# A hashed-attention and two-layer feed-forward kernel: two tiles for the compared bits, another first pair of PSUM banks, and six weight operations in other steps

## The chip, the cores and the metric

The kernel runs on one NeuronCore of one Trainium2 chip. The metric is the time of one execution in microseconds (us) on the device. PE is TensorE (matrix products and transposes), DVE is VectorE, ACT is ScalarE, POOL is GpSimd, and SP is the engine whose queue issues most of the transfers (DMAs). The unit of on-chip result memory that PE writes is a PSUM bank; there are eight.

## The reference

```python
# attention: q, k, v (2, 8, 768, 64), proj (64, 6)
q_bits = (np.einsum('bhsd,dk->bhsk', q, proj) > 0).astype(np.int64)
k_bits = (np.einsum('bhsd,dk->bhsk', k, proj) > 0).astype(np.int64)
powers = 2 ** np.arange(n_bits)
mask = q_bucket[:, :, :, None] == k_bucket[:, :, None, :]   # bucket = sum(bits * powers)
scores = np.where(mask, scale * np.matmul(q, k.transpose(0, 1, 3, 2)), -1000000000.0)
scores = scores - np.max(scores, axis=-1, keepdims=True)
attn = np.exp(scores)
attn = attn / (np.sum(attn, axis=-1, keepdims=True) + 1e-09)
attn_out = np.matmul(attn, v)
# x = attn_out as (1536, 512) tokens; two feed-forward layers, w_in (512, 2048), w_out (2048, 512)
x = np.maximum(x @ w_in, 0.0) ** 2 @ w_out
h = x @ w2_in
out = (h * (1.0 / (1.0 + np.exp(-h)))) @ w2_out
```

The weights of the feed-forward layers arrive as 64-bit floats and are turned into 32-bit floats on the chip.

## The kernel before

**Attention.** The 16 heads are taken as eight pairs (pair 0 to 7). A pair has two heads and each head's queries are taken in two halves of 384 rows, so there are four units `u` per pair and 32 in all. One unit is three blocks of 128 queries against 768 keys. The order of the work is written out by hand: a loop over a step `d` emits, for each step, the row maximum of one block of scores (`row_max`, L984, DVE), two tiny DVE operations (`row_live`, L988 and L989), six transposes of 128x128 into two PSUM tiles `t` (`transp`, L1013, PE), their rounding on ACT (`t_hi`, L1018) and the remainder on DVE (`t_lo`, L1024), four products with v (`av`, L1037 and L1038, PE), the exponential (L997, ACT), and the four products of the next block of scores (`score_mm`, L977, PE). One block of scores per step, so twelve steps per pair, and steps 0 to 95 hold the transposes.

**The bits.** The mask is added by the score product itself: 12 rows of sign bits per head stand below the 64 rows of q and k in the operand tiles `qq` and `kk`. For pair p = 2 to 7, with d0 = 12(p-1), the eight small products of the bits go into one tile `t` of PSUM at the end of step d0-2 (`bits_mm`, L786; this step also does one `t_lo` early). In step d0-1, right behind `row_live`, DVE compares them into the tile `bt` (`bits_cmp`, L791). Pair 1 has its compare in step 2. SP copies `bt` into `qq` and `kk` with four transfers for each head (`place_bits`, L910): for the first head in step d0+2, for the second in step d0+8. The scores use them from step d0+7 and d0+13. SP issues its transfers in order; each one also waits for the landing of the one eight before it. The tile `bt` has one buffer, and so the compare of pair p+1 (step d0+11) needs the last of the four transfers of pair p's second head to have landed. PSUM tiles `t` have three buffers; while the bits wait in one of them, the transposes of the second step behind them wait for it.

**The w_in tiles.** The first four tiles of the first layer's w_in (128x512 each, i = 0 to 3) are converted during the attention: a load (`w_load`), ACT's absolute value (`w_abs`), POOL's limits (`w_limit`), and three DVE operations: `w_exp` (L946), `w_sign` (L950) and `w_low` (L954). The table `W_STEPS` gives for each tile the steps of load, absolute value, `w_exp`, `w_sign` and `w_low`. The DVE operations stand in the list `mid[d]`, between `row_live` and the step's first `t_lo`. In the step of `w_low` of tiles 0 and 1, POOL splits the tile into two parts in `wpa` (`wp_put`, L961 and L962).

**The feed-forward layers.** `moe` records its operations in a planner with costs and due times, which sets the order on every engine; for PE it keeps the written order. The list `idle` hands out the PSUM banks, first in first out. Its first products (`plain`, L420) take 512 tokens at a time: four groups of 12 products, each group in a bank of its own, then the next 512 tokens. The eight tiles `bank0` to `bank7` lie over the attention's PSUM tiles: `bank0` and `bank1` over the first buffer of the scores tile `s`, `bank2` and `bank3` over the second, `bank4` to `bank6` over the `t` tiles and `bank7` over `o`. The last unit's output o31 is put into the first buffer of `s`, where DVE adds its two halves (L1045) at the very end of the attention. Behind the last products with v, PE makes six transposes of the last pair's row sums (L1277), and then the first L420 follows.

Of the kernel before, what the change touches and what calls it, by code (L numbers as in the profile page):

```python
# [11 lines left out]
F32 = mybir.dt.float32  # L12
F32R = mybir.dt.float32r
# [4 lines left out]
ALU = mybir.AluOpType  # L18
# [3 lines left out]
B, H, S, D = 2, 8, 768, 64  # L22
# [4 lines left out]
QW = 384  # L27
KT = S // 128
SCALE = D**-0.5
NBR = 2 * NB  # L30
# [7 lines left out]
W_LO = float(np.uint32(897 << 20).view(np.float32))  # L38
W_HI = float(np.uint32((1150 << 20) | 0xFFFFF).view(np.float32))
V_LAG = 4  # L40
W_STEPS = ((0, 5, 17, 29, 53), (8, 17, 41, 65, 77), (22, 29, 41, 92, 93), (54, 65, 92, 96, 96))
WA = 4
FB = 4
NP = FB // 2
# [175 lines left out]
def moe(nc, t):  # L220
# [11 lines left out]
        count[name] += 1  # L232
        return i

    idle = [0, 1, 4, 7, 2, 3, 5, 6]
    cells = list(range(NCELL))
    early = list(t["early"])

# [411 lines left out]
    for m in range(2):  # L650
        for f in range(NFB):
# [3 lines left out]
            elif m + f == 0:  # L655
                for h in range(2):
                    o = wpa[1][:, :, 4 * h : 4 * h + 4]
# [42 lines left out]
def lsh_attention_moe_moe(ctx, tc, kd, qk, qf, fq, v, pc, wi1, wo1, wi2, wo2, out):  # L700
    nc = tc.nc
# [16 lines left out]
    a1 = att.enter_context(tc.tile_pool(name="a1", bufs=1))  # L718
    a2 = att.enter_context(tc.tile_pool(name="a2", bufs=2))
# [11 lines left out]
    tm = [tmt[:, 2 * i : 2 * i + 2] for i in range(4)]  # L731
# [4 lines left out]
    pair = {}  # L736
# [50 lines left out]
        return o  # L787

    def bits_cmp(p, o):
        t = pair[p]["bt"] = a1.tile([128, S], F32R, tag="bt", name=f"bt{p}")  # L790
        nc.vector.tensor_scalar(out=t[:, 0:QW], in0=o[:, 0:QW], scalar1=tm[0][:, 0:1], scalar2=tm[0][:, 1:2], op0=ALU.is_gt, op1=ALU.mult)  # L791


    first = {}

# [108 lines left out]
    def place_bits(p, h):  # L904
        t = pair[p]
        for n, x in enumerate(("qq", "kk")):
            o = t[x][h][64 : 64 + NBR, 1, :].rearrange("r (z c) -> r z c", z=2)
            for z in range(2):
                r = 64 * n + 32 * z + NBR * h
                nc.sync.dma_start(out=o[:, z].bitcast(F32), in_=t["bt"][r : r + NBR, 0:QW].bitcast(F32))  # L910

    def load_v(p):
        t = pair[p]
# [196 lines left out]
    def at(g, fn, *a):  # L1110
        todo[g].append((fn, a))

    for p in range(1, NPAIR):
        d0 = 12 * (p - 1)
        if p > 1:
            at(d0 - 10, load_pair, p)
            at(d0 - 9, load_k, p)
            at(d0 - 4, new_hi, p)
            at(d0 - 4, cast_pair, p, 1)
            at(d0 - 3, split_pair, p, 1)  # L1120
            scale[d0 - 2] = p
            at(d0 - 2, cast_pair, p, 0)
            at(d0 - 1, split_pair, p, 0)
        else:
            at(0, split_pair, p, 0)
            at(0, split_pair, p, 1)
        long[max(d0 - 2, 1)] = p
        at(d0 + 1, load_head, p, 0)
        at(d0 + 2, place_lo, p, 0)
        at(d0 + 2, place_bits, p, 0)  # L1130
        at(d0 + 5, load_v, p)
        at(d0 + 8, split_v, p)
        at(d0 + 7, load_head, p, 1)
        at(d0 + 8, place_lo, p, 1)
        at(d0 + 8, place_bits, p, 1)
# [14 lines left out]
    for k, d in enumerate(X_STEPS):  # L1150
        at(d, x_form, k)
    for i, (d_load, d_abs, *d_dve) in enumerate(W_STEPS):
        key = (0, 0, i)
# [12 lines left out]
    with tc.manual_schedule():  # L1166
# [17 lines left out]
            out=pdx, in0=k[:, 0:NBR].unsqueeze(1).broadcast_to([128, 2, NBR]), in1=k[:, NBR : 3 * NBR].rearrange("p (a b) -> p a b", a=2), op=ALU.mult  # L1184
# [43 lines left out]
        for d in range(-5, G // 2 + 3):  # L1228
# [10 lines left out]
            if 0 <= g < G and d in (92, 94):  # L1239
                t = ps_s.tile([128, 2, 512], F32, tag="s", name=f"t{g}")  # L1240
# [25 lines left out]
            if d in long:  # L1266
                mid[d + 1].append((bits_cmp, (long[d], bits_mm(long[d]))))
# [5 lines left out]
        p = NPAIR - 1  # L1273
        for z in (1, 0):
            t = ps_t.tile([128, 512], F32, tag="t", name=f"rb{p}_{z}")
# [12 lines left out]
        t = dict(yf=yf, xk=xk, wpa=wpa, raw=raws, wt=wt, pair=both, src=((wi1, wo1), (wi2, wo2)), out=out)  # L1288
# [8 lines left out]
        ops = ("ACT", 0.68, w_abs), ("DVE", 0.43, w_limit), ("DVE", 0.43, w_exp), ("DVE", 0.7, w_sign), ("DVE", 0.7, w_low)  # L1297
        t["first"] = [[(eng, c, partial(fn, key)) for eng, c, fn in ops] for key in early]
        moe(nc, t).emit()


# [45 lines left out]
```

## Time and profile before

| what | value |
|---|---|
| three runs, median (lowest to highest) | 730.95 us (727.33 to 731.03) |
| the profiled execution, time and span | 731.64 us, span 729.9 us |
| mean granted TensorE clock | 0.995 of full speed |
| PE busy | 712.2 us (98%) |
| DVE, ACT, POOL busy | 604.9, 539.7 and 257.6 us |
| attention, until PE's last work of it | 0 to 234 us of the span |
| feed-forward layers | 236.6 us to the end |

A span is counted from the first instruction to the last. The times of rows are counted from the span's start. PE's busy time is modelled and counts overlapping matmuls, so that a high share doesn't say that PE runs at its peak; what PE loses is better read from the distance of equal instructions.

### The profile page before, as it was taken

To read this page: it belongs to the slowest core of one execution; us is meant where nothing else is said; L and a number is where in the kernel's file an instruction comes from. 1 tells how busy PE (TensorE), PEld (TensorE's weight loads), DVE (VectorE), ACT (ScalarE), POOL (GpSimd) and SP (SyncE) were. 2 spreads that over 40 slices of the span, in tenths; PEclk is the share of its full clock that TensorE was granted. 3 is DMA by queue.
4 is the path that set the end of the run, shared out by engine and by line. 5 is a ranking of instruction groups with operands and counts; after the bars stand their busy time and mean duration, and the time that the engine had idled before them with its cause. 6 is when DMAs were issued, how large, how long until landed. Compare 5 with 4: busy or idle time off the path is not lost.

```text
span 729.9 us, 10863 instructions
## 1 busy us (share of the span) xinstructions
PE 712.2 (98%) x3610; PEld 604.8 (83%) x3610; DVE 604.9 (83%) x1099; ACT 539.7 (74%) x1012; POOL 257.6 (35%) x239
## 2 busy tenths in 40 slices
PE   9999999979998999999999999999999999999998
PEld 4988988979897888888887888888788888888887
DVE  7989998969999879786887889989788788978840
ACT  6989998969897798477468558878766855864861
POOL 7635574555746503031232223145203210212300
PEclk9999999999999999999999999999999999999999
DMA  5767868758663337224535553378231331345432
GB/s 170 213 159 195 216 158 190 203 129 201 144 155 84 89 104 173 83 73 102 128 88 115 119 116 106 94 151 167 73 129 58 88 87 62 127 101 116 101 101 101
DMA packets 39496, 92.53 MB, mean 127 GB/s; under 512 B 5944, under 2 KB 11588, under 8 KB 39440
## 3 DMA queue, kind: packets, MB, share of 16 engines
q1 hardware_dynamic: 26976, 67.58, 31.6%
q0 software_dynamic: 12032, 23.79, 18.4%
q8 instruction: 29, 0.48, 0.3%
q10 hardware_dynamic: 432, 0.46, 0.2%
q14 instruction: 27, 0.22, 0.1%
HBM read 52.32 MB, written 3.19 MB: 76 GB/s over the span
## 4 chain that ended last, share of the span: by engine, by line
PE 77%; DVE 11%; SPq 4%; DMA 4%; issue 2%; ACT 1%; POOL 0%; DVEq 0%; ACTq 0%; POOLq 0%
PE bank L558 35%; PE bank L443 23%; PE bank L420 7%; DVE mt L984 4%; DVE tl L1024 4%; PE s L977 4%; PE t L1013 4%; DMA kk<-bt 2%; PE o L1037 2%; PE o L1038 2%; SPq L910 2%; DMA rx<-in_dram 1%; DMA cell<-cell 1%; SPq L766 1%; PE warm L968 1%
## 5 line engine op out<-in xcount | busy, mean ns | idle before, releaser
L558 PE MATMUL bank<-woh,cell 128*128 128x512 f32 (+1 forms) x392 | 120.0, 385 | 0.0
L558 PE MATMUL bank<-cell,woh 128*128 128x512 f32 x384 | 118.5, 389 | 0.2 <-DMA cell<-cell 0.2
L997 ACT ACTIVATE P<-s,mt 128x768 f32<-128x768 f32 x96 | 95.5, 995 | 12.1 <-DVE mt L989 10.3
L1024 DVE TENSOR_TENSOR tl<-t,th 128x384 fp32r<-128x384 f32 x192 | 104.1, 548 | 0.2
L984 DVE TENSOR_REDUCE mt<-s 128x1 f32<-128x768 f32 x96 | 91.3, 951 | 3.1 <-PE s L977 2.1
L1018 ACT CAST th<-t 128x384 fp32r<-128x384 f32 x192 | 82.7, 483 | 14.0 <-PE t L1013 13.9
L1013 PE MATMUL t<-ident,P 128*128 128x128 f32 x576 | 82.3, 276 | 9.7 <-DVE bt L791 8.3
L1013 PEld LDWEIGHTS t<-ident,P 128*128 128x128 f32 x576 | 67.5, 141 | 21.6 <-DVE bt L791 10.2
L558 PEld LDWEIGHTS bank<-woh,cell 128*128 128x128 f32 x392 | 73.2, 188 | 14.7
L558 PEld LDWEIGHTS bank<-cell,woh 128*128 128x128 f32 x384 | 72.1, 188 | 15.6 <-DMA cell<-cell 0.7
L977 PE MATMUL s<-kk,qq 76*128 76x384 f32 (+1 forms) x384 | 83.5, 339 | 0.5 <-ACT P L997 0.5
L278 DVE TENSOR_TENSOR cell<-bank,cell 128x512 f32<-128x512 f32 x91 | 62.1, 692 | 18.7 <-PE bank L443 14.4
L443 PE MATMUL bank<-xw,wpb 128*128 128x512 f32 x312 | 75.9, 389 | 0.0
L558 PE MATMUL bank<-wol,cell 128*128 128x512 f32 (+1 forms) x196 | 75.4, 385 | 0.0
L558 PE MATMUL bank<-cell,wol 128*128 128x512 f32 x192 | 74.7, 389 | 0.0
L1037 PE MATMUL o<-th,vv 128*128 128x384 f32 x192 | 73.1, 381 | 0.0
L977 PEld LDWEIGHTS s<-kk,qq 76*128 76x128 f32 (+1 forms) x384 | 68.1, 189 | 2.2 <-ACT P L997 1.6
L443 PEld LDWEIGHTS bank<-xw,wpb 128*128 128x128 f32 x312 | 58.5, 188 | 12.4 <-DVE bank L278 0.3
L1038 PE MATMUL o<-tl,vv 128*128 128x384 f32 x192 | 65.1, 339 | 0.0
L588 ACT COPY yf<-bank 128x512 f32<-128x512 f32 x48 | 27.9, 586 | 34.6 <-PE bank L558 34.0
L450 ACT COPY cell<-bank 128x512 f32<-128x512 f32 x39 | 22.9, 586 | 40.6 <-PE bank L443 38.6
L268 ACT CAST cell<-cell 128x512 fp32r<-128x512 f32 x81 | 48.8, 617 | 2.7 <-DMA cell<-cell 1.6
(185 smaller groups left out, 1456.0 us busy)
## 6 DMA issues: line engine op xcount, KB each, us to landing
raw<-in_dram SPq DMA_DIRECT2D x62, 512.0 KB
cell<-cell POOLq DMA_DIRECT2D x23, 256.0 KB, 4.0
qq<-hq SPq DMA_DIRECT2D x28, 192.0 KB
kk<-in_dram POOLq DMA_DIRECT2D x14, 384.0 KB, 4.5
yf<-cell POOLq DMA_DIRECT2D x21, 256.0 KB, 3.3
vr<-in_dram SPq DMA_DIRECT2D x8, 384.0 KB
ta<-ob SPq DMA_DIRECT2D x31, 96.0 KB
tb<-ob SPq DMA_DIRECT2D x31, 96.0 KB
```

What stands on the lines that cost most here:

```text
L278: add("DVE", 0.70, lambda: vec.tensor_tensor(out=val(out), in0=bank[b], in1=val(other), op=ALU.add), [("bank", b), *reads], writes)
L420: mm(bank[b], wpa[n][:, p, 4 * h + j], x[:, q], start=j == 0 and z == 0, stop=j == 3 and z == 2)
L443: mm(bank[b], w[:, p], x[:, q], start=not started and z == 0, stop=z == 2, skip_group_check=started)
L558: mm(bank[b][:, 0:wd], x, y, start=start and i == 0 and z == 0, stop=i == (FB if half is None else 2 * half + 2) - 1 and z == 2, skip_grou ...
L977: mm(s[:, n, 0:QW], t["qq"][h][0:kk, ab, c0 : c0 + 128], t["kk"][h][0:kk, ab, n * QW : (n + 1) * QW], start=ab == 0, stop=ab == 1)
L984: nc.vector.tensor_reduce(out=m[:, 0:1], in_=s[:, :, 0:QW], op=ALU.max, axis=AX.XY, negate=True)
L997: nc.scalar.activation(out=e.rearrange("p (a b) -> p a b", a=2), in_=s[:, :, 0:QW], func=AF.Exp, scale=m[:, 1:2], bias=m[:, 2:3], accum_ou ...
L1013: nc.tensor.transpose(t[:, j * 128 : (j + 1) * 128], P[u, j][:, kt * 128 : (kt + 1) * 128], ident)
L1018: nc.scalar.copy(out=th, in_=PT[g][0][:, 0:QW])
L1024: nc.vector.tensor_tensor(out=tl, in0=t[:, 0:QW], in1=th.bitcast(F32), op=ALU.subtract)
L1037: mm(o[:, 0:QW], vv, th, start=kt == 0, stop=False)
L1038: mm(o[:, 0:QW], vv, tl, start=False, stop=kt == KT - 1)
```

## The change

The compare writes tiles `bn` of 384 columns from a pool with two buffers, where it wrote the one buffer `bt` (768 columns, of which 384 were used). The list `idle` starts with banks 2 and 3 and has 0 and 1 in their place. Six DVE operations on the w_in tiles 0 and 1, and one on tile 2, stand in other steps; with `w_low`, the two operations of `wp_put` on POOL move as well. The loads, ACT's and POOL's first operations keep their steps.

```diff
-W_STEPS = ((0, 5, 17, 29, 53), (8, 17, 41, 65, 77), (22, 29, 41, 92, 93), (54, 65, 92, 96, 96))
+W_STEPS = ((0, 5, 10, 22, 34), (8, 17, 46, 58, 70), (22, 29, 46, 92, 93), (54, 65, 92, 96, 96))
...
-    idle = [0, 1, 4, 7, 2, 3, 5, 6]
+    idle = [2, 3, 4, 7, 0, 1, 5, 6]
...
     def bits_cmp(p, o):
-        t = pair[p]["bt"] = a1.tile([128, S], F32R, tag="bt", name=f"bt{p}")
-        nc.vector.tensor_scalar(out=t[:, 0:QW], in0=o[:, 0:QW], scalar1=tm[0][:, 0:1], scalar2=tm[0][:, 1:2], op0=ALU.is_gt, op1=ALU.mult)
+        t = pair[p]["bt"] = a2.tile([128, QW], F32R, tag="bn", name=f"bn{p}")
+        nc.vector.tensor_scalar(out=t, in0=o[:, 0:QW], scalar1=tm[0][:, 0:1], scalar2=tm[0][:, 1:2], op0=ALU.is_gt, op1=ALU.mult)
...
-                nc.sync.dma_start(out=o[:, z].bitcast(F32), in_=t["bt"][r : r + NBR, 0:QW].bitcast(F32))
+                nc.sync.dma_start(out=o[:, z].bitcast(F32), in_=t["bt"][r : r + NBR].bitcast(F32))
```

On DVE, this is the place of pair 2's compare (steps 10 and 11) before the change. In brackets stand the semaphores that an instruction waits for; DMAHW are those of SP's transfers.

```order
L1024 TENSOR_TENSOR tl20_631<-t20_625,th20_629 128x384 [waits Activation_49]
L1024 TENSOR_TENSOR tl21_647<-t21_633,th21_637 128x384 [waits Activation_49]
L984 TENSOR_REDUCE mt_92<-s5_0_651 128x1 [waits PE_49]
L988 TENSOR_SCALAR mt_92<-mt_92 128x1 [waits DVE_49]
L989 TENSOR_SCALAR mt_92<-mt_92 128x1
L791 TENSOR_SCALAR bt2_666<-bs2_656,tmt_88 128x384 [waits DMAHW3_49,DMAHW4_49,DMAHW2_49,DMAHW5_49,DMAHW1_49,PE_49]
L1024 TENSOR_TENSOR tl22_674<-t22_668,th22_672 128x384 [waits Activation_49]
```

The same place of DVE after the change (the lines behind L790 have a number that is lower by one), with `w_exp` of tile 0 ahead of step 10's remainders:

```order
L945 TENSOR_SCALAR wi0_288<-wi0_288 128x512 [waits Pool_49]
L1023 TENSOR_TENSOR tl20_632<-t20_626,th20_630 128x384 [waits Activation_49]
L1023 TENSOR_TENSOR tl21_648<-t21_634,th21_638 128x384 [waits Activation_49]
L983 TENSOR_REDUCE mt_92<-s5_0_652 128x1 [waits PE_49]
L987 TENSOR_SCALAR mt_92<-mt_92 128x1 [waits DVE_49]
L988 TENSOR_SCALAR mt_92<-mt_92 128x1
L791 TENSOR_SCALAR bn2_667<-bs2_657,tmt_88 128x384 [waits PE_49]
L1023 TENSOR_TENSOR tl22_675<-t22_669,th22_673 128x384 [waits Activation_49]
```

The compare now waits for PE alone (from pair 3 on also for transfers of two pairs before), and a w_in operation has come in six rows ahead of it; the same holds for the compares in steps 23, 35, 47, 59 and 71, with two such operations ahead of the one in step 47.

On PE, this is the place between the attention's last transposes (`rb`) and the first products of the feed-forward part before the change:

```order
L1277 MATMUL rb7_0_3739<-ident_86,rw7_3671 128x128 [waits PE_49]
L1277 MATMUL rb7_0_3739<-ident_86,rw7_3671 128x128 x2
L420 MATMUL bank0_3764<-xk_59,wpa0_60 128x512 [waits DVE_49]
L420 MATMUL bank0_3764<-xk_59,wpa0_60 128x512 x11
L420 MATMUL bank1_3765<-xk_59,wpa0_60 128x512 x12
L420 MATMUL bank4_3768<-xk_59,wpa1_61 128x512 [waits Activation_49]
L420 MATMUL bank4_3768<-xk_59,wpa1_61 128x512
L420 MATMUL bank4_3768<-xk_59,wpa1_61 128x512 [waits DVE_49]
L420 MATMUL bank4_3768<-xk_59,wpa1_61 128x512 x9
```

The same place of PE after the change:

```order
L1276 MATMUL rb7_0_3739<-ident_86,rw7_3671 128x128 [waits PE_49]
L1276 MATMUL rb7_0_3739<-ident_86,rw7_3671 128x128 x2
L420 MATMUL bank2_3766<-xk_59,wpa0_60 128x512 x12
L420 MATMUL bank3_3767<-xk_59,wpa0_60 128x512 x12
L420 MATMUL bank4_3768<-xk_59,wpa1_61 128x512 [waits PE_49,Activation_49]
L420 MATMUL bank4_3768<-xk_59,wpa1_61 128x512
L420 MATMUL bank4_3768<-xk_59,wpa1_61 128x512 [waits DVE_49]
L420 MATMUL bank4_3768<-xk_59,wpa1_61 128x512 x9
```

The first wait for DVE now stands 24 products later, at the weights of `wpa1`. In the rest of the feed-forward part the banks 0 and 2, and 1 and 3, have changed places; the order on every engine is otherwise the same.

## Rows read from the trace of the kernel before

**Rows 1.** The page: busy time, share of the span and instructions of each engine.

```profile
PE 712.2 (98%) x3610; PEld 604.8 (83%) x3610; DVE 604.9 (83%) x1099; ACT 539.7 (74%) x1012; POOL 257.6 (35%) x239
```

**Rows 2.** Waits, us in total, times, longest: DVE and PE in the attention.

```profile
DVE bt L791 <- DMA kk<-bt: 10.4, 5, 4.5
PE t L1013 <- DVE bt L791: 8.3, 6, 3.9
```

**Rows 3.** Timeline of PE, steps 10 to 14: start, length, instruction; idle before in brackets.

```profile
37.03 0.82 PE L1013 MATMUL t<-ident,P 128*128 128x128 f32 x6
39.96 0.87 PE L1013 MATMUL t<-ident,P 128*128 128x128 f32 x6
...
43.86 1.01 PE L1013 MATMUL t<-ident,P 128*128 128x128 f32 x6 [1.61 <-DVE bt L791]
...
46.11 0.82 PE L1013 MATMUL t<-ident,P 128*128 128x128 f32 x6
...
48.17 0.82 PE L1013 MATMUL t<-ident,P 128*128 128x128 f32 x6
```

**Rows 4.** Timeline of PE, steps 59 to 61.

```profile
149.89 0.88 PE L1013 MATMUL t<-ident,P 128*128 128x128 f32 x6
...
151.30 0.88 PE L977 MATMUL s<-kk,qq 128*128 128x384 f32 x4
156.11 1.54 PE L1013 MATMUL t<-ident,P 128*128 128x128 f32 x6 [3.93 <-DVE bt L791]
...
159.50 0.82 PE L1013 MATMUL t<-ident,P 128*128 128x128 f32 x6
```

**Rows 5.** Timeline of DVE in step 2, pair 1's compare.

```profile
21.29 0.67 DVE L791 TENSOR_SCALAR bt<-bs,tmt 128x384 fp32r<-128x384 f32 x1
```

**Rows 6.** Timeline of PE, steps 78 and 79, of DVE in step 77.

```profile
197.15 0.49 PE L1013 MATMUL t<-ident,P 128*128 128x128 f32 x3
...
199.70 0.82 PE L1013 MATMUL t<-ident,P 128*128 128x128 f32 x6
...
196.71 0.68 DVE L954 SCALAR_TENSOR_TENSOR wi<-raw,wi 128x512 uint32<-128x512 uint32 x1
197.31 0.55 DVE L1024 TENSOR_TENSOR tl<-t,th 128x384 fp32r<-128x384 f32 x1
```

**Rows 7.** Line L946 on DVE: shortest, median, longest ns; first and last start.

```profile
L946 DVE TENSOR_SCALAR wi<-wi x2: 415/416/417, 56.1 to 110.0; 128x512 uint32<-128x512 uint32 x2
```

**Rows 8.** Timeline of SP, pair 5's first head: start, length of issue.

```profile
135.63 1.90 SPq L910 DMA_DIRECT2D kk<-bt  x2
```

**Rows 9.** The chain that ended last, 141 to 156 us: start, length, what.

```profile
141.05 9.10 DMA rx<-in_dram
...
151.73 3.52 DMA kk<-bt
```

**Rows 10.** Timeline of PE at the end of the attention.

```profile
233.15 0.84 PE L1277 MATMUL rb<-ident,rw 128*128 128x128 f32 x6
236.61 14.15 PE L420 MATMUL bank<-xk,wpa 128*128 128x512 f32 x54 [2.62 <-DVE ta L1045]
250.59 1.52 PE L420 MATMUL bank<-xw,wpa 128*128 128x512 f32 x6
251.95 1.52 PE L420 MATMUL bank<-xk,wpa 128*128 128x512 f32 x6
```

**Rows 11.** Timeline of DVE at the same place.

```profile
235.99 0.56 DVE L1045 TENSOR_TENSOR ta<-o,ta 64x384 f32<-64x384 f32 x1
...
237.62 2.37 DVE L261 TENSOR_TENSOR wpa<-both,wpa 128x512 fp32r<-128x512 f32 x2
```

**Rows 12.** Stretches: us; busy (instructions) of PE, PEld, DVE, ACT, POOL; granted clock, DMA share, GB/s.

```profile
70.90:97.70 26.80, 26.32 (x177) 24.30 (x177) 25.85 (x65) 24.71 (x54) 16.48 (x16) 1.00 0.85 205
...
236.60:240.20 3.60, 3.59 (x10) 2.85 (x11) 3.52 (x5) 1.68 (x4) 1.66 (x1) 0.60 0.00 0
240.20:244.00 3.80, 3.80 (x17) 3.10 (x16) 2.44 (x5) 2.32 (x5) 2.53 (x3) 0.93 0.39 69
```

## Prediction

> **What bounds the kernel now.** The page comes first: PE is busy 98% of the span and no other engine over 83% [rows 1]. So what PE does without a gap can't get shorter by this change, which takes no instruction from PE; a gain has to come from gaps and from steps that are longer than PE's work. The waits come next. In the attention DVE's compare waits 10.4 us for the landing of `kk<-bt`, and PE's transposes wait 8.3 us in six places for that compare [rows 2]. Then the timeline of PE gives the length of each step, the distance between the first transposes of two steps. A plain step is 2.06 us (46.11 to 48.17), and a step whose end holds the bits is 2.93, so 0.87 more (37.03 to 39.96) [rows 3]. What is over these lengths is lost. At the end of the attention the timeline shows one more gap, 2.62 us before the first product of the feed-forward part [rows 10].
>
> **The compare's second buffer.** It removes the wait for the transfers of the pair before. In pair 2 the step behind the compare took 3.90 (39.96 to 43.86), 1.84 over a plain one, of which 1.61 is the marked wait; the next took 2.25, 0.19 over [rows 3]. That is 2.03 lost, 0.42 beyond the marked wait: the late compare leaves the remainders late too. In pair 6 the two steps took 6.22 and 3.39, so 4.16 + 1.33 = 5.49 lost, at a marked wait of 3.93; the six transposes behind it took 1.54 where 0.82 is usual, so PE's clock had fallen too [rows 4]. The other four have 8.3 - 1.61 - 3.93 = 2.76 of marked wait, and with 0.42 more for each, 4.44. The six together: 2.03 + 5.49 + 4.44 = 11.96 us.
>
> Is the compare free when it doesn't wait? Pair 1's, in step 2, started without any idle time of DVE [rows 5]. It covers some 0.6 us of DVE, and the 0.87 us that PE spends on the bits hides it; without that cover it would cost up to 0.6 six times. I count nothing for it. What was late behind the wait was PE's next use of the third `t` buffer; once the compare is on time, the next thing that can be late is the bits' own arrival in `qq` and `kk`, which the scores need. The tightest is the second head of pair 5: SP's load of a w_in tile took 9.10 us to land, the transfer eight places later waited for it, and the last `kk<-bt` landed at 151.73 + 3.52 = 155.25 [rows 9]. The scores of step 61 use it in their second half, 1.41 us behind the step's start (149.89 to 151.30) [rows 4] plus two products, some 0.35. With plain steps from 149.89 on, that is 149.89 + 4.12 + 1.76 = 155.77; step 53 loses its w_in operation (about 0.5 earlier) and step 58 gains one (below, about 0.3 later), so about 155.55. The transfer is 0.3 us early: I count nothing, with a bound of 1 us. The next tightest that I found is pair 5's first head: issued by 137.53 [rows 8], and even with the slowest landing of these rows, 3.52, there at 141.05; needed in step 55, which starts four steps ahead of 149.89 (2.93 + 3 x 2.06 = 9.11, so at 140.78), at 142.54. 1.5 us of room.
>
> **The moved w_in operations.** DVE's six places cost now what the last of them shows: an operation that takes DVE 0.60 (196.71 to 197.31) made a step of 2.55 (197.15 to 199.70), so 0.49 lost [rows 6]. The five before it, read the same way, lost 0.23 (one short operation of 0.42 [rows 7]), 0.50, 0.58 (two short ones), 0.48 and 0.49: 2.77 in all. DVE has thus little room, about 0.1 us in a plain step. In the new place each stands one step ahead of a compare. There DVE has 0.60 + 0.60 more to do, PE 0.87: 0.33 of it isn't hidden, less some 0.05 to 0.1 of room, so I take 0.28 for each of the four long operations; for the short one 0.05; for step 46 with two short ones 0.40. Sum 1.57, and a gain of 2.77 - 1.57 = 1.20. Bounds: all hidden, a gain of 2.77; none hidden, as in the places before, 0. `wp_put` moves on POOL to steps 34 and 70, ahead of a subtraction that isn't used before step 38 or 74; POOL is busy 35% [rows 1], and I count nothing. If that cover failed, the low parts of pairs 4 and 7 would be later by these two operations, and PE would lose what that is over their room at the scores.
>
> **The banks.** The first product waits for DVE's last addition of o31 (L1045), which ends at 236.55 [rows 11], as it writes where o31 lies. With bank 2 it waits for nothing, so it can follow the transposes, which end at 233.99: the gap of 2.62 goes [rows 10]. The clock goes with it: after the gap it was 0.60 of full speed for 3.6 us and 0.93 for the next 3.8 [rows 12], so most of the first stretch ran at 1.2 GHz. The first 54 products took 13.98 us (236.61 to 250.59); the next six took 1.36 (250.59 to 251.95), 0.2267 each, and at that pace 54 take 12.24. So 1.74 more is lost there and comes back: 4.36 together. What is late next: the third group of 12 needs `wpa1`, which DVE writes from 237.62 to 239.99, half by about 239 [rows 11]. PE comes to it at 233.99 + 24 x 0.2267 = 239.43, and to the other half at 242.15; it is hidden by 0.4 us at least. Bounds: all of the 4.36, or, if PE stands there as long as it does now, nothing.
>
> The Trainium skill (TensorE: Matmul & The Clock Gate, What's actually happening) calls the number of matmuls at the low clock variable from run to run, and advises not to fit one. By that the 1.74 wouldn't be counted and the time would be 1.7 us longer; the rows show the loss in this execution, and I count it.
>
> **The sum.** 11.96 + 1.20 + 4.36 = 17.5 us. The profiled execution took 731.64 us, 0.7 over the median of the three runs; 731.64 - 17.5 = 714.1, and I say 714.0. The rest of the feed-forward part stays as long as it is: PE has no other gap of note there.
>
> **The rivals.**
> *The wait moves to the scores.* The compare no longer holds the steps back, and SP's queue, which is in order, doesn't get faster; the late landing then stops PE at the scores of pair 5's second head. For it: the room there is 0.3 us, and DMA engines were busy 0.85 of one pair's stretch [rows 12]. Against it: the other deadlines have 1.5 us and more. If the load lands 2 us later, PE waits 1.7 and loses some 1.4 more to the clock and the late remainders as in pair 6, and pair 5's first head costs 0.5: 714 + 3.6 = 717.6. Chance 0.12. The Trainium skill (DMA: Bandwidth & Descriptors, Issuing engines are not separate DMA queues) says that transfers from all engines run on the same 16 DMA engines and interleave. That speaks for this rival; no row here separates it from SP's order.
> *The start of the feed-forward part stays where it is*, because PE is stopped at `wpa1`, whose DVE operations run beside POOL's and vary. 4.36 isn't gained: 718.4. Chance 0.10.
> *The w_in operations are no better hidden*: 1.2 isn't gained, 715.2; it lies in the forecast's own range, chance 0.15.
> *Slower than before.* One mechanism: the transfers of the bits become the bound. Each of seven pairs would have to land so late that PE loses (17.5 + 3.65)/7 = 3.0 us at its scores, so with 1.5 us of room, 4.5 us later than now. From there on the time is over 734.6. The DMA share of 0.85, at 26.80 us for a pair, becomes 0.89 at 25.6 (12 x 2.06 + 0.87), and stays below one. Chance 0.02.
> *The change doesn't do what it says*: a compare that still waits. Its wait is now for transfers issued some 15 steps before, 31 us, so only 0.01; it would leave 726.
>
> **How the numbers follow.** The forecast itself, 712 to 716.5, has 0.75 with the third rival in it; the remaining 0.25 are the others. The range goes down to 710.5: all moved operations hidden (-1.6), and the runs shown lie up to 3.7 apart, of which I take half. It goes up to 718.5, which takes in the lost start. A measurement of this kernel can tell 0.5%, 3.65 us, from no change, so faster means below 727.3: 0.95, for the stall alone takes more than that; the same 0.03, slower 0.02.
>
> **What would show it.** Right: no wait of PE for L791; steps of 2.06 behind the compares; 2.93 to 3.3 for the steps with bits and a w_in operation together with the one behind; L420 right behind the last transposes at full clock. Wrong: PE waiting at L977 for `kk<-bt`, steps behind the compares of 2.5 and more, or a gap at the third group of L420. The prediction fails if the transfers land later once the steps are shorter, or if DVE's lag in the steps with bits carries on into the next ones.

## The result, and the profile after

The changed kernel took 720.46 us (median of four runs, 718.87 to 723.0), the kernel before 730.99 beside it (four runs, 727.33 to 731.75). The ratio is 0.9869, with a 95% interval from 0.9825 to 0.9913: faster by 1.3%, 9.6 us. The prediction said 714.0 and at most 718.5; the time lies 2.0 us above the range. The profiled execution took 719.92 us, 11.7 less than the profiled one before (731.64).

In the changed kernel the transposes are L1012, the remainders `tl` L1023, `w_sign` L949, `w_low` L953.

The page of the changed kernel, the lines that answer to [rows 1]:

```profile
span 718.1 us, 10858 instructions
PE 707.4 (99%) x3610; PEld 602.1 (84%) x3610; DVE 612.7 (85%) x1099; ACT 539.1 (75%) x1012; POOL 258.9 (36%) x239
```

DVE has as many instructions as before, 1099, yet is busy 612.7 us where it was 604.9. No instruction was added, so some of the old ones take longer: 7.8 us in all.

The changed kernel's waits of PE and of DVE in the attention (20 to 226 us), which answer to [rows 2]: us in total, times, longest.

```profile
PE t L1012 <- DVE tl L1023: 5.5, 5, 1.3
DVE mt L983 <- PE s L976: 0.3, 1, 0.3
```

Both old rows are gone: DVE no longer waits for a transfer at L791, PE no longer for the compare. PE never waits at the scores for `kk<-bt` either. But a new row has come: in five places the transposes wait for DVE's remainders. A moved w_in operation stands ahead of the remainders in each of the six steps with bits (10, 22, 34, 46, 58, 70); the five are all of these but step 10, which has one short operation. Here is the first of the five, steps 22 to 26, on the timeline of PE:

```profile
64.95 0.52 PE L786 MATMUL bs<-rq,pjs 128*32 128x384 f32 x2
...
67.04 1.01 PE L1012 MATMUL t<-ident,P 128*128 128x128 f32 x6 [1.24 <-DVE tl L1023]
...
69.37 1.01 PE L1012 MATMUL t<-ident,P 128*128 128x128 f32 x6
71.62 0.82 PE L1012 MATMUL t<-ident,P 128*128 128x128 f32 x6
73.68 0.49 PE L1012 MATMUL t<-ident,P 128*128 128x128 f32 x3
```

The step that ends at 67.04 began at 62.80, so it took 4.24 where 2.93 is usual [rows 3]; the next two took 2.33 and 2.25, then 2.06 again. So 1.31 + 0.27 + 0.19 = 1.77 are lost at this place. Read the same way, the six places lose 0.07, 1.77, 1.74, 1.06, 1.67 and 1.68: 7.99 us, where the prediction had 1.57.

What DVE and POOL do there, on the changed kernel's timeline:

```profile
64.40 0.20 DVE L988 TENSOR_SCALAR mt<-mt 128x1 f32<-128x1 f32 x1
64.52 2.00 DVE L949 SCALAR_TENSOR_TENSOR wi<-rx,wi 128x512 uint32<-128x512 uint32 x1
66.44 1.01 DVE L1023 TENSOR_TENSOR tl<-t,th 128x384 fp32r<-128x384 f32 x2
64.14 1.83 POOL L774 TENSOR_TENSOR lp<-rk,hk 128x768 fp32r<-128x768 f32 x1
66.06 0.52 POOL L1054 TENSOR_SCALAR sums<-sums 128x12 f32<-128x12 f32 x1
```

An operation that took 0.68 in the old places [rows 6] takes 2.00. It started 0.38 after a subtraction of POOL (`split_pair`, the low parts of the next pair) that ran from 64.14 to 65.97, and it ended at 66.52, 0.55 after it. That is nearly its own length, counted from the end of POOL's. The other three long operations look alike, each beside the same subtraction of 1.83 and ending some 0.55 behind it, by DVE's groups (busy us, mean ns):

```profile
L953 DVE SCALAR_TENSOR_TENSOR wi<-rx,wi 128x512 uint32<-128x512 uint32 x1 | 2.0, 2043 | 0.0
L949 DVE SCALAR_TENSOR_TENSOR wi<-raw,wi 128x512 uint32<-128x512 uint32 x1 | 2.0, 1971 | 0.0
L953 DVE SCALAR_TENSOR_TENSOR wi<-raw,wi 128x512 uint32<-128x512 uint32 x1 | 1.9, 1916 | 0.0
```

The start of the feed-forward part, on the changed kernel's chain that ended last (start, length, what), answers to [rows 10]:

```profile
226.61 0.66 PE rb L1276 x6
227.26 32.67 PE bank L420 x144
```

and its stretches (columns as in [rows 12]):

```profile
226.40:230.00 3.60, 3.60 (x20) 3.09 (x20) 3.40 (x4) 1.71 (x3) 1.79 (x2) 1.00 0.47 153
230.00:234.00 4.00, 4.00 (x20) 3.30 (x19) 4.00 (x6) 3.24 (x7) 1.68 (x1) 1.00 0.00 2
```

The products follow the transposes without a gap, and the granted clock is 1.00, the level of 2.4 GHz, where it was 0.60 before.

### The profile page after: what moved, and what is told of

Its sections match the earlier page's. It is cut to its first block, busy times and chain, and to the rows that moved or that the text cites. A ratio compares the mean times of both kernels' runs of the same rounds, so it can differ in the third digit from the quotient of the medians.

```text
span 718.1 us, 10858 instructions
## 1 busy us (share of the span) xinstructions
PE 707.4 (99%) x3610; PEld 602.1 (84%) x3610; DVE 612.7 (85%) x1099; ACT 539.1 (75%) x1012; POOL 258.9 (36%) x239
## 4 chain that ended last, share of the span: by engine, by line
PE 88%; DVE 9%; POOL 1%; DMA 0%; issue 0%; ACT 0%; POOLq 0%; DVEq 0%
PE bank L558 36%; PE bank L443 25%; PE bank L420 7%; PE t L1012 7%; PE s L976 6%; PE o L1036 4%; PE o L1037 3%; DVE mt L983 3%; DVE tl L1023 3%; DVE wi L949 1%; DVE wi L953 1%; DMA fc<-in_dram 0%; DVE mt L988 0%; POOL kk L855 0%; POOL vv L920 0%
## 5 line engine op out<-in xcount | busy, mean ns | idle before, releaser
L996 ACT ACTIVATE P<-s,mt 128x768 f32<-128x768 f32 x96 | 95.6, 996 | 12.1 <-DVE mt L988 9.5
L1023 DVE TENSOR_TENSOR tl<-t,th 128x384 fp32r<-128x384 f32 x192 | 103.9, 547 | 0.2
L1012 PE MATMUL t<-ident,P 128*128 128x128 f32 x576 | 80.9, 274 | 5.5 <-DVE tl L1023 5.5
L1012 PEld LDWEIGHTS t<-ident,P 128*128 128x128 f32 x576 | 67.1, 140 | 16.1 <-DVE tl L1023 11.4
```

Source lines behind the costliest of these rows:

```text
L996: nc.scalar.activation(out=e.rearrange("p (a b) -> p a b", a=2), in_=s[:, :, 0:QW], func=AF.Exp, scale=m[:, 1:2], bias=m[:, 2:3], accum_ou ...
L1012: nc.tensor.transpose(t[:, j * 128 : (j + 1) * 128], P[u, j][:, kt * 128 : (kt + 1) * 128], ident)
L1023: nc.vector.tensor_tensor(out=tl, in0=t[:, 0:QW], in1=th.bitcast(F32), op=ALU.subtract)
```

## The experiments

Two theories for the missing 6 us. Theory 1: POOL's subtraction and DVE's w_in operation shut each other out, so the operation takes what is left of the subtraction and its own time. Theory 2: DVE just has no room in the steps with bits, and any operation there delays PE.

**e_banks**: the kernel before with the order of banks alone.

```
-    idle = [0, 1, 4, 7, 2, 3, 5, 6]
+    idle = [2, 3, 4, 7, 0, 1, 5, 6]
```

> The kernel before with the other half of the banks first, nothing else. Both theories: the gap of 2.62 us ahead of the first product of the feed-forward part goes, and the 1.74 that the low clock costs behind it: 4.4 us less, about 726.6, ratio 0.994. If PE is stopped at the third group's weights instead, no change, 731.0.

Measured: 726.78 us, ratio 0.9956 (0.9929 to 0.9982), so 3.2 us less (1.3 to 5.2). PE has no wait left at L420, and the products begin behind the transposes. The predicted 4.36 lies in the interval, and so does the 2.62 of the gap alone.

**e_bits**: the kernel before with the second buffer alone (the part of the diff in `bits_cmp` and in the load of the bits).

> The kernel before with the second buffer for the compared bits alone. By the prediction's sum 11.96 us, so 719 us and a ratio of 0.984; the w_in operations then lose what they lose before, 2.77, and the gap ahead of the feed-forward part stays, 2.6 us. Rival: part of the 11.96 is given back as waits at the scores for the transfers of the bits (1 to 3.6 us, so 720 to 723, ratio 0.985 to 0.989). By the runs so far, 715.6 for this together with the banks and 4.2 for the banks alone, 719.8 (0.985).

Measured: 718.41 us, ratio 0.9857 (0.9825 to 0.9888), so 10.4 us less (8.2 to 12.7); predicted were 11.96. All six steps with bits are 2.92 or 2.93, those behind them 2.12 or 2.13, and the next 2.04 or 2.05, so the compare's wait leaves nothing behind, and nothing is given back at the scores. Its gap ahead of the feed-forward part is still there, with the row of waits

```profile
PE bank L420 <- DVE ta L1044: 2.2, 1, 2.2
```

Behind this gap, though, the clock didn't fall: the granted clock was 1.00, as the stretch and the chain of this kernel show.

```profile
224.80:228.40 3.60, 3.56 (x16) 2.95 (x17) 3.48 (x5) 2.16 (x5) 1.68 (x1) 1.00 0.00 0
224.84 32.94 PE bank L420 x144
```

**e_oldsteps**: the changed kernel with the w_in operations in their old places.

```
-W_STEPS = ((0, 5, 10, 22, 34), (8, 17, 46, 58, 70), (22, 29, 46, 92, 93), (54, 65, 92, 96, 96))
+W_STEPS = ((0, 5, 17, 29, 53), (8, 17, 41, 65, 77), (22, 29, 41, 92, 93), (54, 65, 92, 96, 96))
```

> The changed kernel with the table of steps of before: two buffers for the bits and the other banks, the w_in operations in their old places. Both theories: the old places cost 2.77 us and the new ones 7.99, so 5.2 less than the changed kernel, about 715.2, ratio to before 0.979. No step with bits longer than 2.95. If the miss had another cause than the moved operations, this would stay near 720.

Measured: 715.64 us, ratio 0.9804 (0.9777 to 0.9831). So the table alone costs the changed kernel about 0.65%, 4.8 us, where the prediction gave it a gain of 1.2. The steps with bits are 2.93 again. POOL's subtraction still runs beside DVE there, and DVE's own work is not held up by it, as its timeline in this kernel shows:

```profile
64.91 1.01 DVE L1023 TENSOR_TENSOR tl<-t,th 128x384 fp32r<-128x384 f32 x2
63.69 1.85 POOL L774 TENSOR_TENSOR lp<-rk,hk 128x768 fp32r<-128x768 f32 x1
```

The remainders read one operand, `t`, from PSUM, and two of them take 1.01 with the subtraction (to 65.54) or without it.

**e_steps**: the kernel before with the moved w_in operations alone.

> The kernel before with the moved w_in operations alone. In the places before, 2.77 us are won back. Theory 1, POOL's subtraction holds them back in the new places by about 1.4 each: the compare behind them in steps 35, 59 and 71 waits for transfers already, for 0.5 to 3.9 us, so up to that wait their lateness costs nothing; I expect 4 us lost of the 8 in the changed kernel, and 731 - 2.8 + 4 = 732 (ratio 1.002; from 0.998 to 1.007). Theory 2, no room in the steps but no more than 0.3 an operation: 731 - 2.8 + 0.5 = 728.7 (0.997). Whichever, long operations of about 2 us in steps 23, 35, 59 and 71 speak for theory 1.

Measured: 730.36 us, ratio 1.0021 (0.9999 to 1.0043). In the kernel before the move costs little, since the compare waits for transfers behind it anyway. Its waits of PE in the attention:

```profile
PE t L1013 <- DVE bt L791: 5.3, 4, 2.2
PE t L1013 <- DVE tl L1024: 4.5, 4, 1.6
```

Part of the old 8.3 us [rows 2] has turned into waits for remainders. The long operations took 1.00, 0.76, 1.92 and 2.25 us; only two of the four came near 2 us or over it, the two that started beside the subtraction L774; the other two met the end of another subtraction of POOL's. The three parts alone add to -10.4 + 1.5 - 3.2 = -12.1 us against -9.6 for all; each is uncertain by some 2 us, so the runs can't tell that difference from none. But the table's own price, 1.5 us here (its interval reaches zero) and 4.8 once the wait is gone (e_oldsteps), goes the way that the traces show.

**e_ksplit**: the changed kernel with the subtraction taken away from beside the w_in operation.

```
-            at(d0 - 3, split_pair, p, 1)
             scale[d0 - 2] = p
             at(d0 - 2, cast_pair, p, 0)
+            at(d0 - 1, split_pair, p, 1)
             at(d0 - 1, split_pair, p, 0)
```

> The changed kernel, with one edit: POOL's subtraction for the low part of k moves from step d0-3 to step d0-1, ahead of that for q, so that POOL doesn't subtract while DVE has its w_in operation in the steps with bits. Theory 1 (POOL's subtraction and the DVE operation shut each other out): the operations L949 and L953 of tiles 0 and 1 take 0.68 us again, where they took 1.92 to 2.04; the steps 23, 35, 59 and 71 and the two behind each lose 0.3 instead of 1.7, step 47 and the two behind it 0.4 instead of 1.06; 6.0 us less than the changed kernel, about 714.0, ratio to before 0.977. Theory 2 (DVE has no room in the steps with bits, whatever POOL does): as the changed kernel, 720.5, ratio 0.987, and the operations' places cost 1.7 each as now.

Measured: 716.51 us, ratio 0.9814 (0.9786 to 0.9842). The four long operations stand in the same steps as in the changed kernel and are short again, by DVE's groups (busy us, mean ns):

```profile
L949 DVE SCALAR_TENSOR_TENSOR wi<-raw,wi 128x512 uint32<-128x512 uint32 x1 | 0.8, 778 | 0.0
L953 DVE SCALAR_TENSOR_TENSOR wi<-rx,wi 128x512 uint32<-128x512 uint32 x1 | 0.7, 683 | 0.0
L953 DVE SCALAR_TENSOR_TENSOR wi<-raw,wi 128x512 uint32<-128x512 uint32 x1 | 0.7, 683 | 0.0
L949 DVE SCALAR_TENSOR_TENSOR wi<-rx,wi 128x512 uint32<-128x512 uint32 x1 | 0.7, 679 | 0.0
```

The steps 22, 34, 58 and 70 (the expectation counts them by their compare, one higher) took 2.93, 2.93, 3.02 and 2.92; here are the first and the one behind it on the timeline of PE:

```profile
62.88 0.82 PE L1012 MATMUL t<-ident,P 128*128 128x128 f32 x6
...
65.81 1.00 PE L1012 MATMUL t<-ident,P 128*128 128x128 f32 x6
```

So theory 2 falls as the main cause. But it has a part in it: each of the four places still loses 0.37 to 0.48, nearly all of it in the two steps behind (2.24 to 2.32 each), where the prediction had 0.28. The time is 2.5 us over theory 1's 714.0, and the profiled execution shows where. About 0.6 is this. About 1.1 is step 46, which lost 1.5 where 0.4 was expected: its two short operations took 0.81 and 1.04, the first beside a subtraction of POOL, the second beside a cast. The third part is at the end of the attention, where POOL was held up and PE waited for it:

```profile
221.40 0.68 DVE L949 SCALAR_TENSOR_TENSOR both<-rx,both 128x512 uint32<-128x512 uint32 x1
221.43 1.34 POOL L1061 COPY rw<-sums 128x768 f32<-128x768 f32 x1
222.82 0.88 PE L1276 MATMUL rb<-ident,rw 128*128 128x128 f32 x6 [0.84 <-POOL rw L1061]
```

POOL's copy took 0.82 in the kernel before; here it started 0.03 after DVE's operation and took 1.34. It is theory 1 with the parts exchanged.

**e_onein**: the changed kernel in which the four long operations read one tile instead of two. They mask or shift the raw word and set a constant bit; the joining is left out.

```
-        nc.vector.scalar_tensor_tensor(out=tu, in0=hi, scalar=0xC0000000, in1=tu, op0=ALU.bitwise_and, op1=ALU.bitwise_or)
+        nc.vector.tensor_scalar(out=tu, in0=hi, scalar1=0xC0000000, scalar2=0x20000000, op0=ALU.bitwise_and, op1=ALU.bitwise_or)
...
-        nc.vector.scalar_tensor_tensor(out=tu, in0=lo, scalar=29, in1=tu, op0=ALU.logical_shift_right, op1=ALU.bitwise_or)
+        nc.vector.tensor_scalar(out=tu, in0=lo, scalar1=29, scalar2=0x20000000, op0=ALU.logical_shift_right, op1=ALU.bitwise_or)
```

> The changed kernel in which the four long w_in operations of the tiles 0 and 1 read one tile of SBUF instead of two (they mask or shift the raw word and set a constant bit; the joining with the words formed before is left out, so the weights of the feed-forward part are other numbers). Their places, beside POOL's subtraction, stay. Theory 1a: an operation of DVE and one of POOL shut each other out only where DVE reads two tiles of SBUF; then these four take 0.6 or less, the steps 23, 35, 59 and 71 lose about 0.45 each with the two behind them, as with POOL's subtraction moved, in place of 6.86 together, and the kernel takes 720.5 - 5.1 = 715.4 (ratio 0.980). Theory 1b: any operation of DVE from SBUF to SBUF of this size is shut out; they take about 2 us, and the time stays at 720.5 (0.987). Theory 2, DVE has no room in these steps: the operations are 0.1 shorter, 4 x 0.1, so 720 (0.987).

Measured: 719.18 us, ratio 0.9869 (0.9838 to 0.9901). Neither 1a nor 1b came out: two of the four operations were short and two long, by the order of their starts. The timeline of DVE and POOL in this kernel, steps 22 and 34:

```profile
64.58 0.45 DVE L950 TENSOR_SCALAR wi<-rx 128x512 uint32<-128x512 uint32 x1
64.81 1.90 POOL L774 TENSOR_TENSOR lp<-rk,hk 128x768 fp32r<-128x768 f32 x1
...
90.30 1.84 POOL L774 TENSOR_TENSOR lp<-rk,hk 128x768 fp32r<-128x768 f32 x1
90.47 1.95 DVE L957 TENSOR_SCALAR wi<-rx 128x512 uint32<-128x512 uint32 x1
```

In step 22 DVE started 0.23 ahead of POOL and took 0.45; in step 34 it started 0.17 after POOL and took 1.95. The same holds for steps 70 (0.42, ahead by 0.18) and 58 (1.82, behind by 0.29). Where DVE came first, the place lost 0.21 and 0.18 us, where POOL came first, 1.65 and 1.52. These are the clearest rows for theory 1, inside one execution: whoever starts first keeps the way, and one tile read from SBUF is enough. Theory 2 can't tell these places apart. The kernel's time stayed near that of the changed one since step 46 now met the subtraction: one of its short operations took 2.04 and the place lost 2.62, so that the six places together still lost 6.2 of the 7.99.

**e_vsplit**: the changed kernel with the long operations one step earlier (21, 33, 57, 69), beside POOL's subtraction of `vv` in steps without bits, and the short ones back in step 41.

```
-W_STEPS = ((0, 5, 10, 22, 34), (8, 17, 46, 58, 70), (22, 29, 46, 92, 93), (54, 65, 92, 96, 96))
+W_STEPS = ((0, 5, 17, 21, 33), (8, 17, 41, 57, 69), (22, 29, 41, 92, 93), (54, 65, 92, 96, 96))
```

> The changed kernel with the four long w_in operations in the steps 21, 33, 57 and 69: no bits and no compare in the same or the next step but one, but POOL subtracts there for the low part of v; the short ones in steps 17 and 41 as before. Theory 1: these four operations take 1.2 to 1.5 us in the trace and each place loses 1.0 to 1.3 us instead of 0.5, so some 2.8 more than with the old table, about 718, ratio 0.982. Theory 2: they take 0.68 and lose 0.5 each, as with the old table, 715.2, ratio 0.979.

Measured: 719.73 us, ratio 0.9861 (0.9834 to 0.9889). Without bits in the step the operations still took 0.97, 1.55, 1.83 and 2.30 us, so it is POOL's subtraction, not the compare. Each ended 0.54 or 0.55 behind the end of the subtraction; this is the third:

```profile
142.97 1.83 POOL L920 TENSOR_TENSOR vv<-vr,vv 128x768 fp32r<-128x768 f32 x1
143.51 1.83 DVE L949 SCALAR_TENSOR_TENSOR wi<-raw,wi 128x512 uint32<-128x512 uint32 x1
```

The time is 1.7 us over theory 1's figure: the delay reached the steps with bits behind (3.81 to 6.67 where 2.93 is usual). In the longest PE's clock fell as well, to 0.55 and 0.60 of full speed in the 4 us (174 to 178 us) behind a wait of 1.99.

**e_best**: the changed kernel with the edit of e_ksplit and the short operations back in step 41.

> The changed kernel with POOL's second subtraction of a pair one step before the pair instead of three, as before, and the short w_in operations back in step 41. Theory 1: the four long operations take 0.68 and lose about 0.45 each with the steps behind, 1.8 together; step 47 loses nothing (1.5 with POOL's subtraction moved), step 41 loses 0.6. So 716.5 - 0.9 = 715.6, ratio 0.980, the same within the measurement as with all operations in their old places (715.6). Theory 2: no better than the changed kernel less the short ones' 1.06, 719.4 (0.985).

Measured: 715.25 us, ratio 0.9814 (0.9783 to 0.9846), the same as with the old table. Step 46 lost 0.06. The long operations took 1.22, 0.84, 1.15 and 0.68, though; the first three now met a shorter work of POOL, the cast `hk` (0.82). One row pair of this kernel shows what POOL doesn't hold up:

```profile
146.99 0.68 DVE L791 TENSOR_SCALAR bn<-bs,tmt 128x384 fp32r<-128x384 f32 x1
146.86 1.83 POOL L774 TENSOR_TENSOR lp<-rk,hk 128x768 fp32r<-128x768 f32 x1
```

The compare reads PSUM; it started 0.13 after the subtraction and took its usual 0.68.

## Why the prediction was wrong

**The step that failed** is the price of the moved w_in operations: "In the new place each stands one step ahead of a compare. There DVE has 0.60 + 0.60 more to do, PE 0.87 [...] so I take 0.28 for each of the four long operations". The sum over the six places was 1.57 us and measured 7.99. The 0.60 was taken from [rows 6], a place where POOL does nothing. In the new places POOL subtracts, and a long operation takes about 2 us. Put into the prediction's own sum, the error of 7.99 - 1.57 = 6.42 closes the gap: 714.1 + 6.4 = 720.5, measured 720.46. That it closes so exactly is luck, for the two other terms measured less alone than the sum has (10.4 for 11.96, 3.2 for 4.36), and the sum starts from an execution 0.7 over the median. The bounds failed as well: the "none hidden, as in the places before, 0" was no lower bound, for a place can be worse than the old one.

The cause is shown from three sides: with the subtraction moved away (e_ksplit) the operations are 0.68 to 0.78 in the same steps; with another subtraction of POOL in other steps (e_vsplit) they are long there; and with a shorter form (e_onein) the same operations beside the same subtraction are short or long by which of the two starts first. What the reader of the trace before could have seen are these rows, which the prediction didn't look for. The first is POOL's subtraction in the stretch from step 22 (64.97) to step 23 (67.90); the others are a w_in operation of the same form at the end of the attention.

```profile
65.39 1.84 POOL L774 TENSOR_TENSOR lp<-rk,hk 128x768 fp32r<-128x768 f32 x1
...
233.02 2.39 POOL L1083 TENSOR_TENSOR ta<-ta,tb 64x384 f32<-64x384 f32 x2
...
233.64 2.32 DVE L954 SCALAR_TENSOR_TENSOR both<-rx,both 128x512 uint32<-128x512 uint32 x1
```

The same L954 took 0.68 in [rows 6] and 2.32 beside POOL, to 235.96, 0.55 behind the end of POOL's two (235.41). That was the price of the new places, in the old trace: what is over PE's room, 2.0 + 0.60 - 0.87 - 0.1 = 1.6, comes near the 1.67 to 1.77 that each of the four lost.

The Trainium skill (SBUF — State Buffer, SBUF: two separate sides) states it as a rule: DVE and GpSimd share a port pair that is an exclusive lock, taken for the whole instruction by whichever starts first, and on DVE's side by operations in a two-port mode or, against an operation of GpSimd that reads SBUF, with two SBUF inputs. The rows agree in both orders of start (0.45 and 1.95 us in e_onein), and in that remainders and compares, which read one operand from PSUM, are free of it (0.55 and 0.68 beside POOL). Whether the form that reads one tile runs in a two-port mode no row here shows.

**A second miss, smaller:** even where POOL hardly holds it up (0.68 to 0.78 in e_ksplit) a long operation ahead of a compare costs 0.37 to 0.48, not 0.28, since DVE's lag carries on into the two steps behind. The prediction named that as what would make it fail, and priced it at nothing. The four together are 1.75, so even then the table would have won at most 2.77 - 1.75 = 1.0, less what the short ones cost. The runs couldn't tell so little from none: e_best (715.25) and e_oldsteps (715.64) come out the same.

**The compare's second buffer** was right. The wait is gone, the steps behind are plain, nothing moved to the scores. It measured 10.4 us (8.2 to 12.7) alone, against 11.96 read from one execution.

**The banks** were right in the gap, and the clock's part was that of one execution. The gap of 2.62 is gone, and the first 144 products of L420 took 32.67 where the kernel before's same row of the chain has

```profile
236.61 34.55 PE bank L420 x144
```

so 1.88 came back behind the gap (1.74 were counted): 4.5 in the profile, 3.2 (1.3 to 5.2) in the runs of e_banks. But the clock doesn't fall in every execution. In the profiled ones of e_bits and e_steps, with gaps of 2.2 and 2.3, it stayed at 1.00 and the same products took 32.94. Three executions of the kernel before, run beside the experiments (726.08, 726.58 and 726.6 us), have a mean granted clock of 1.000; a fall as in [rows 12] would bring it to 0.998. So the 1.74 is lost in some executions only, where the sum counts it as certain, and the runs of e_banks can't tell a gain of 2.6 from one of 4.4.

**The rivals:** PE waits neither at the scores nor at `wpa1`, and the compare doesn't wait. "The w_in operations are no better hidden" was the right place with the wrong size: it stopped at a loss as before, 2.77.

## What to carry to other kernels

Before an operation is moved on DVE, look at what POOL does at the new place, not only at how busy DVE and PE are: an operation from SBUF to SBUF that starts behind one of POOL takes what is left of that plus most of its own time, and the share of busy time (POOL 35%) says nothing on it. Price it by a row of the same form beside a busy POOL, if the trace has one, and let the bounds reach below "as before". A move that looks harmless while a wait stands behind it (e_steps, 1.5 us) can cost more once that wait is removed (4.8).

## What the runs showed of the hardware

DVE's 128x512 operations on SBUF took 0.42 to 0.68 us alone. In the changed kernel and e_onein they took 1.82 to 2.04 when they started 0.13 to 0.46 after a subtraction of POOL of 1.83 to 1.88. They ended some 0.55 behind it when they read two tiles and 0.28 when they read one, so the wait is hidden in their own busy time and no row of waits names POOL. The order of the starts decides for one tile read as well (0.45 or 1.95). Started first, DVE keeps its time and POOL pays: its subtraction that started 0.22 before DVE's end took 1.90 instead of 1.83, its copy that started 0.65 before DVE's end took 1.34 instead of 0.82. Remainders and compares, which read PSUM, run beside POOL at their usual 0.55 and 0.68. A gap of PE of 2.62 was followed by a granted clock of 0.60 in one execution, gaps of 2.2 and 2.3 in two others by 1.00.
